# Batch 0 of an RWKV-to-Fourier kernel: fills and table halves on ScalarE, one masked state update per chunk, and a new written-out order

## The chip, the cores and the metric

The kernel runs on one core of a Trainium2 chip. The metric is device time in microseconds of one execution. The engines of the core work side by side, each through its own queue of instructions in order: TensorE (PE in the profile, its weight loads PEld), VectorE (DVE), ScalarE (ACT), GpSimd (POOL) and SyncE (SP), which issues nearly all DMAs.

## The reference

Two layers follow one another. The first is a linear attention with a state that decays channel by channel; the second mixes all tokens and channels of a batch by a two-dimensional Fourier transform (real part), normalises, and applies a two-layer MLP. B, H, S, D = 4, 8, 768, 48.

```
for t in range(S):
    kt, vt, rt, wt = k[:, :, t], v[:, :, t], r[:, :, t], w[:, :, t]
    cur = einsum('bhd,bhe->bhde', u[None] * kt, vt)
    y[:, :, t] = einsum('bhd,bhde->bhe', rt, state + cur)
    state = wt[..., None] * state + einsum('bhd,bhe->bhde', kt, vt)
x = y.transpose(0, 2, 1, 3).reshape(B, S, H * D)        # 4 x 768 x 384
u = x + real(fft(fft(x, axis=1), axis=2))
un = (u - mean(u)) / sqrt(var(u) + 1e-6)                 # over the 384 channels
out = u + maximum(un @ w_ch1, 0) @ w_ch2                 # 384 -> 1536 -> 384
```

## The kernel before, in words

**Tiling.** The tokens of a batch are cut into six chunks of 128, so that there are 24 chunks; chunk c of batch b is called b.c here. A chunk's w, k, r and v come in as four loads of 192 KB each (`in_w`, `in_k`, `in_r`, `in_v`, seven buffers of each), all issued by SP in one row. The attention of a chunk goes: the logarithm of w (`lb`, ACT), cumulative sums of it by matmuls with masks (L567, L571, and per-head totals at L577, PE), exponentials (ACT), r and k times these (`rh`, `kh`, on DVE for batch 0; `kh` on POOL from batch 1 on), transposes (PE) and their eviction (`rtb`, `ktb`, ACT), the 128x128 products (L637, PE), their masking (`ah`, DVE), the new state (L652 and L654, PE; `st`, DVE), the output (L672 and L676, PE), and the diagonal term from r, k, u and v (`rk` twice and `vtd` on POOL, `dc` on DVE; in batch 0 it is added by a float32 matmul at L684). The result goes to `x` (L688 on ACT in batch 0, L690 on DVE later). Two heads share the 128 partitions: the state tile is 128 x 4 x 96, and only the half of each 96 that belongs to the own head may be other than zero.

**Mixing and MLP.** `x` is folded into sums and differences (`xf`), multiplied with cosine and sine tables `cs` and `ss` (L732), evicted to `hcs` (L736), mirrored (`hcr`, POOL), multiplied with the channel tables `dtm` and `dtp` (L749), added to x (L751), normalised (`un`), transposed and evicted (`unt`, L771). Then come the two MLP layers: L790 with its evictions `ht` (L799 on ACT, L795 on DVE), and L809, whose result goes through `osb` (L814, DVE) to the output. L790 needs `w1` and L809 needs `w2`, which POOL loads in two DMAs of 1152 KB.

**Tables.** `cs` and `ss` are made in the kernel: DVE reduces the angles (194 columns for each of three row blocks), ACT takes the sines, and DVE mirrors each quarter with a sign per partition (`sgb`, `sgs`; four tensor_scalar operations in `mirrors`). `tables_end` fills row blocks 3 to 5 from blocks 0 to 2, once copied and once negated (four DVE operations, 576 to 579 columns), and makes `dtm` and `dtp`.

**Order.** Every operation is recorded once with its dependences. `ORDER` is a list of all operation numbers, written out by a planner outside the kernel; each engine executes its own operations in that order, and `BANKS` gives the PSUM bank of each new tile. Waits between engines follow from the dependences. A stalled operation holds all behind it on its engine. Twenty pairs of matmuls without use (L851, "warm") are strewn into PE's row in the first stretch.

Of the kernel before, what the change touches and what calls it, by code (L numbers as in the profile page):

```python
# [75 lines left out]
]  # L76
BANKS = (
    "01023402567432053245243260745603275063543257020560726405702501027615453276601650465325701327363601540235701357"
    "04317420370154237015470231754315236571632451764356437565361014234761032604371461376035427610312521521125761532"
    "65713675431647153265723102752407562716304571641350730473601457632701647546320165460154603546210654106235461676"  # L80
    "0173275410326754104326710543040236745012362"
)
# [203 lines left out]
def bass_rwkv6_finch__then__fnet_fourier_mix_kernel(  # L286
# [119 lines left out]
    def fill(o, val):  # L406
        return lambda e: e.memset(o, val)
# [477 lines left out]
```

## Time and profile before

| | before |
|---|---|
| median of 3 runs | 209.9 us (209.96, 209.9, 208.45) |
| profiled execution, its own time | 208.6 us |
| span of the profile | 206.7 us |
| PE / DVE / ACT / POOL busy | 186.8 / 154.6 / 140.8 / 121.5 us |
| mean granted TensorE clock | 0.989 of full speed |
| loads and stores moved | 26.26 MB |

The span runs from the first to the last instruction; the profiled execution's own time has 1.9 us around it. "Busy" on PE counts the warm matmuls too (L851, 11.1 us in all). In the first quarter of the span PE is not full: in the 40 slices of the page its busy tenths begin 3599957798799999.

### The profile page before, as it was taken

The page shows a single profiled execution, that of the slowest core. Times are in us where ns is not written, and L with a number is a line of the kernel's source. Part 1 is how long each engine was busy: PE and PEld are TensorE (multiplying, and loading weights), DVE is VectorE, ACT ScalarE, POOL GpSimd, SP SyncE. Part 2 cuts the span into 40 slices and gives each one's busy share as a digit, 9 for nine tenths or more (in the row PEclk, how much of TensorE's full clock was granted, in tenths as well). Part 3 has the DMA queues.
Part 4 walks back from the last instruction along what each step waited for, and adds up shares of the span by engine and source line. Part 5 has one row for each costly group of instructions (what it writes and reads, how often), then busy time and mean ns, then how long its engine had stood idle before and what let it go on. Part 6 is the DMA issues. An engine that isn't in the chain of part 4 may idle for free.

```text
span 206.7 us, 4611 instructions
## 1 busy us (share of the span) xinstructions
PE 186.8 (90%) x1760; PEld 116.4 (56%) x1760; DVE 154.6 (75%) x344; ACT 140.8 (68%) x325; POOL 121.5 (59%) x152
## 2 busy tenths in 40 slices
PE   3599957798799999898999999999999999999994
PEld 0255634453466666575666666766566666656652
DVE  7789998387745899999996589999648994823403
ACT  3898843455999997586996695669956613883530
POOL 5777876435479998785999998992011483000000
PEclk9999999799999999999999999999999999999998
DMA  6999999999999999989929910210110101201203
GB/s 119 220 217 205 196 185 166 166 205 203 187 213 217 183 223 203 226 177 233 209 76 186 195 41 3 76 41 0 38 41 0 43 30 50 75 4 38 76 3 114
DMA packets 105273, 26.26 MB, mean 127 GB/s; under 512 B 100257, under 2 KB 104866, under 8 KB 105250
## 3 DMA queue, kind: packets, MB, share of 16 engines
q1 hardware_dynamic: 103298, 23.60, 53.2%
q0 software_dynamic: 1952, 2.36, 7.2%
q8 instruction: 14, 0.23, 0.5%
q14 instruction: 9, 0.07, 0.1%
HBM read 23.59 MB, written 4.72 MB: 137 GB/s over the span
## 4 chain that ended last, share of the span: by engine, by line
PE 41%; DVE 19%; SPq 11%; POOL 10%; ACT 7%; DMA 5%; issue 5%; POOLq 0%; DVEq 0%; ACTq 0%
PE bank L790 14%; PE bank L809 13%; SPq L431 11%; POOL rk L396 5%; DMA in_v<-in_v_dram 5%; DVE ah L642 4%; PE bank L749 3%; DVE xf L396 3%; DVE osb L814 3%; DVE xa L396 2%; DVE st L662 2%; DVE x L690 2%; POOL kh L396 2%; POOL vtd L396 2%; PE bank L637 1%
## 5 line engine op out<-in xcount | busy, mean ns | idle before, releaser
L790 PE MATMUL bank<-unt,w 128*128 128x384 bf16 x288 | 52.9, 326 | 0.6 <-ACT unt L771 0.6
L809 PE MATMUL bank<-w,ht 128*128 128x384 bf16 x288 | 53.1, 326 | 0.0
L799 ACT ACTIVATE ht<-bank 128x384 bf16<-128x384 f32 x80 | 37.0, 497 | 10.2 <-PE bank L790 10.2
L790 PEld LDWEIGHTS bank<-unt,w 128*128 128x128 bf16 x288 | 26.1, 98 | 17.5 <-ACT unt L771 1.0
L809 PEld LDWEIGHTS bank<-w,ht 128*128 128x128 bf16 x288 | 26.8, 98 | 16.1 <-ACT ktb L629 0.2
L642 DVE TENSOR_TENSOR ah<-bank,msk 128x512 bf16<-128x512 f32 x48 | 31.2, 682 | 6.2 <-PE bank L637 6.0
L396 POOL TENSOR_TENSOR vtd<-in_v,dc 128x384 f32<-128x384 f32 x24 | 20.0, 836 | 13.9 <-DVE dc L594 9.0
L396 POOL TENSOR_TENSOR kh<-in_k,e 128x384 bf16<-128x384 f32 x18 | 18.1, 1008 | 15.7 <-ACT e L587 15.7
L396 POOL TENSOR_TENSOR rk<-in_r,in_k 128x384 f32<-128x384 f32 x24 | 24.2, 1008 | 3.5 <-DMA in_r<-in_r_dram 3.2
L396 POOL TENSOR_TENSOR rk<-rk,ub 128x384 f32<-128x384 f32 x24 | 24.2, 1014 | 0.8
L814 DVE SCALAR_TENSOR_TENSOR osb<-bank,rstd,x 128x384 f32<-128x384 f32 x24 | 14.7, 611 | 11.8 <-PE bank L809 11.7
L410 ACT ACTIVATE un<-x,agg 128x384 bf16<-128x384 f32 x24 | 14.5, 617 | 6.9 <-DVE agg L757 6.8
L662 DVE TENSOR_TENSOR st<-bank,e 64x192 bf16<-64x192 f32 x40 | 14.1, 353 | 4.6 <-PE bank L676 2.3
L594 DVE TENSOR_REDUCE dc<-rk 128x8 f32<-128x384 f32 x24 | 13.2, 551 | 5.3 <-POOL rk L396 3.1
L751 DVE TENSOR_TENSOR x<-bank,x 128x384 f32<-128x384 f32 x24 | 12.6, 547 | 5.0 <-PE bank L749 5.0
L629 ACT ACTIVATE ktb<-bank 128x512 bf16<-128x512 bf16 x24 | 14.2, 602 | 2.8 <-PE bank L624 2.7
L627 ACT ACTIVATE rtb<-bank 128x512 bf16<-128x512 bf16 x24 | 14.2, 601 | 2.8 <-PE bank L618 2.4
L602 DVE TENSOR_TENSOR rh<-bank,in_r 128x384 bf16<-128x384 f32 x24 | 13.0, 547 | 3.5 <-ACT bank L573 3.2
L410 ACT ACTIVATE vb<-in_v 128x384 bf16<-128x384 f32 x24 | 12.7, 531 | 2.9 <-DMA in_v<-in_v_dram 2.8
L410 ACT ACTIVATE lb<-in_w 128x384 bf16<-128x384 f32 x24 | 12.6, 528 | 2.6 <-PE bank L567 2.5
L795 DVE TENSOR_SCALAR ht<-bank 128x384 bf16<-128x384 f32 x16 | 8.8, 551 | 7.3 <-PE bank L790 7.1
L587 ACT ACTIVATE e<-bank 128x388 f32<-128x388 f32 (+1 forms) x18 | 9.0, 506 | 7.4 <-PE bank L577 5.9
(116 smaller groups left out, 373.6 us busy)
## 6 DMA issues: line engine op xcount, KB each, us to landing
in_w<-in_w_dram SPq DMA_DIRECT2D x24, 192.0 KB, 3.7
in_k<-in_k_dram SPq DMA_DIRECT2D x24, 192.0 KB, 3.9
in_r<-in_r_dram SPq DMA_DIRECT2D x24, 192.0 KB, 3.8
in_v<-in_v_dram SPq DMA_DIRECT2D x24, 192.0 KB, 3.9
out_dram<-osb SPq DMA_DIRECT2D x24, 192.0 KB, 1.9
w<-in_moe_w_ch_dram POOLq DMA_DIRECT2D x2, 1152.0 KB, 10.6
ht<-in_u_dram SPq DMA_DIRECT2D x1, 1.5 KB
```

The source lines that it names most:

```text
L396: return shared(lambda e: e.tensor_tensor(out=o, in0=a, in1=b, op=f))
L410: return lambda e: e.activation(o, a, f, **kw)
L431: return e.dma_start(INB[n][i][:, :, :], src[n][b, :, c * CH:(c + 1) * CH, :].rearrange("h t d -> t h d"))
L594: op("dve", "dc", lambda e: e.tensor_reduce(out=dc[:, :], in_=rku[:, :, :], axis=mybir.AxisListType.X, op=ALU.add), r=[("RK", i2)], w=[("D ...
L627: op("act", "ev512", lambda e: e.activation(rT[:, :, :].rearrange("p h t -> p (h t)"), psb(trr)[:, 0:512], ACTF.Copy), r=[trr], w=[("RTB", ...
L629: op("act", "ev512", lambda e: e.activation(kT[:, :, :].rearrange("p h t -> p (h t)"), psb(trk)[:, 0:512], ACTF.Copy), r=[trk], w=[("KTB", ...
L642: masked[n] = op("dve", "ah", lambda e, x=x: e.tensor_tensor(out=ah[:, x:H:2, :], in0=ps(ta[x])[:, :].rearrange("p (h t) -> p h t", t=128) ...
L662: op("dve", "st", lambda e, x=x, pr=pr: e.tensor_tensor(out=s_out[pr, :, D * x:D * x + D], in0=ps(tds)[pr, 0:DM].rearrange("p (h d) -> p h ...
L790: ins = e.matmul(ps(t)[:, 0:384], W1[:, m, 128 * j:128 * j + 128], unt[:, m, :], start=(m == 0), stop=(m == NM - 1))
L799: op("act", "ev384", lambda e, j=j, t=t, ht=ht: e.activation(ht[:, j, :], ps(t)[:, 0:384], ACTF.Relu), r=[t], w=[("HT", q % 2, j)])
L809: ins = e.matmul(ps(t)[:, 0:DM], ht[:, j, 128 * x:128 * x + 128], W2[:, j, :], start=(j == 0), stop=(j == NJ - 1))
L814: op("dve", "osb", lambda e, kb=kb, t=t, o=o: e.scalar_tensor_tensor(out=o[:, :], in0=ps(t)[:, 0:DM], scalar=rstd[:, kb:kb + 1], in1=uf[:, ...
```

## The change

1. The zero columns 48 to 63 of every head in `lb`, `rh` and `kh` are filled by ScalarE (a Copy of a broadcast zero, `fill384`) and no longer by GpSimd. The fill of the state tile goes away.
2. In batch 0 the state update becomes one VectorE operation over all 128 partitions and 384 columns (`stm`) in place of two over 64 partitions and 192 columns (`st`). The factor for the half that must be zero is made zero: the totals get a second column per head pair, and a further matmul adds -10000 to the exponent of the entries that don't belong (`totm`, with the new tile `NEGM`).
3. The four mirrors of the tables become tensor_tensor operations, with the sign broadcast as second operand (`mirt`).
4. The four fills of row blocks 3 to 5 go from VectorE to ScalarE (`upa`).
5. `ORDER` and `BANKS` are new throughout.

```diff
     def fills():
-        e = "pool"
         for n, T in (("LB", LBS), ("RH", RHS), ("KH", KHS)):
-            op(e, "fill192", fill(T[:, :, :, D:64].rearrange("p n h d -> p (n h) d"), 0.0), w=[(n, i) for i in range(NB)])
-        op(e, "fill768", fill(STS[:, :, :, :].rearrange("p n h d -> p (n h d)"), 0.0), ...)
+            zero(T[:, :, :, D:64].rearrange("p n h d -> p (n h) d"), NB * H, 64 - D, "fill384", [(n, i) for i in range(NB)], FE[0])
...
+    def zero(o, n, m, kind, w, e="act"):
+        if e == "act":
+            op(e, kind, act(o, ZERO[:, 0:1].unsqueeze(1).to_broadcast([128, n, m]), ACTF.Copy), r=["ZERO"], w=w)
+        else:
+            op(e, kind, fill(o, 0.0), w=w)
...
-            op("dve", "mir", ts(T[:, 0:3, HS:HS - 96:-1], T[:, 0:3, Q:Q + 96], sg[:, :], None, ALU.mult),
+            sgb = sg[:, 0:1].unsqueeze(1).to_broadcast([128, 3, 96])
+            op("dve", "mirt", tt(T[:, 0:3, HS:HS - 96:-1], T[:, 0:3, Q:Q + 96], sgb, ALU.mult),
...
-            op("dve", "up", shared(lambda e, T=T: e.tensor_copy(out=T[:, 3:6, Q:HF], in_=T[:, 0:3, Q:HF])),
-            op("dve", "up", ts(T[:, 3:6, 0:Q], T[:, 0:3, 0:Q], -1.0, None, ALU.mult), r=lo, ...)
+                    op("act", "upa", act(T[:, 3:6, q0:q1], T[:, 0:3, q0:q1], ACTF.Copy, scale=(1.0, -1.0)[x]), r=lo, w=w)
...
+    FE, UPE, MST, HCD = ("act", "pool", "pool", "pool"), ("act", "act"), range(NC), ()
...
                 for h in range(HP):
-                    ins = e.matmul(ps(tci)[:, DM + h:DM + h + 1], L[:, 2 * h:2 * h + 2, :]..., ONE[:, :])
+                    ins = e.matmul(ps(tci)[:, DM + m * h:DM + m * h + m], L[:, 2 * h:2 * h + 2, :]..., ONE[:, 0:m], ...)
+                if mst:
+                    ins = e.matmul(ps(tci)[:, DM:DM + H], IDB[:, :], NEGM[:, :, :].rearrange("p h x -> p (h x)"), start=False, stop=True, ...)
...
+            if mst:
+                op("dve", "stm", lambda e: e.tensor_tensor(
+                    out=s_out[:, :, :].rearrange("p h (x d) -> p h x d", d=D),
+                    in0=ps(tds)[:, 0:DM].rearrange("p (h x d) -> p h x d", d=D, x=2),
+                    in1=we.rearrange("p (h x) -> p h x", x=2).unsqueeze(3).to_broadcast([128, HP, 2, D]), op=ALU.mult),
...
-    66, 7, 0, 3, 1, 6, 8, 38, 67, 2, 36, 68, 5, 9, 39, 69, 70, 10, 22, 102, 16, 37, 103, 17,
...
```

The new order shows at three places. The first is on ScalarE, at the end of batch 0's attention. `vb2<-in_v6` is the bf16 copy of the v of chunk 1.0, the first chunk of the next batch; the rows `x<-` are the outputs of batch 0's chunks, the last of them that of chunk 0.5. Before:

```order
L688 ACTIVATE x<-bank7 128x384
L627 ACTIVATE rtb2<-bank0 128x512
L573 ACTIVATE bank6<-bank6 128x384
L410 ACTIVATE vb2<-in_v6 128x384
L688 ACTIVATE x<-bank2 128x384
L629 ACTIVATE ktb2<-bank5 128x512
L629 ACTIVATE ktb0<-bank0 128x512
L627 ACTIVATE rtb0<-bank7 128x512
L688 ACTIVATE x<-bank0 128x384
```

With the change, from the output of chunk 0.5 on:

```order
L720 ACTIVATE x<-bank3 128x384
L555 ACTIVATE dtp<-bank6,cp 128x384
L594 ACTIVATE bank4<-bank4 128x384
L555 ACTIVATE dtp<-bank3 128x384
L772 ACTIVATE hcs0<-bank5 128x2x193
L553 ACTIVATE dtm<-bank3 128x384
L772 ACTIVATE hcs0<-bank2 128x2x193
L772 ACTIVATE hcs0<-bank1 128x2x193
L553 ACTIVATE dtm<-bank6 128x384
L555 ACTIVATE dtp<-bank6 128x384
L653 ACTIVATE rtb0<-bank2 128x512
L413 ACTIVATE vb2<-in_v6 128x384
```

The copy of v of chunk 1.0 stood ahead of the last two outputs of batch 0; now it stands eleven operations behind the last of them.

The second place is the start of the program, on GpSimd and VectorE. `tc`, `ki`, `ht1` and `tci` are index tables; `tn` and the `ht` rows are the first steps of the angle tables, `sgi` the parity of the partition. GpSimd before, and then with the change:

```order
L413 IOTA ki 128x194
L407 MEMSET kh 128x24x16
L413 IOTA tc 128x6
L407 MEMSET lb 128x24x16
L413 IOTA tci 128x1
L407 MEMSET st 128x768
L407 MEMSET rh 128x24x16
L413 IOTA ht1 128x384
```

```order
L416 IOTA ki 128x194
L416 IOTA tc 128x6
L416 IOTA ht1 128x384
L410 MEMSET xf 128x6x128
L410 MEMSET x 128x18x4
L410 MEMSET xf 128x6x128
L416 IOTA tci 128x1
```

VectorE with the change, at the same place; before, `tn` was followed at once by the five `ht0` rows of the tables:

```order
L403 TENSOR_SCALAR tn<-tc 128x3
L403 TENSOR_SCALAR sgi<-tci 128x1
L403 TENSOR_SCALAR msk<-ht1 128x128
L403 TENSOR_SCALAR idw<-ht1 128x384
L404 TENSOR_SCALAR ht0<-ki,tn 128x194
```

The small table `tci` moved behind three fills on GpSimd, and its reader `sgi`, with two masks behind it, moved ahead of the angle tables on VectorE.

The third place is on GpSimd where the MLP's weights are loaded (the two DMA rows; `vtd3` belongs to chunk 0.3, `rk2` to chunk 0.5, `kh<-in_k6` to chunk 1.0). Before, and then with the change:

```order
L542 DMA w1<-in_moe_w_ch1_dram 128x3x1536
L396 TENSOR_TENSOR xf<-x 128x191
L396 TENSOR_TENSOR vtd3<-in_v3,dc0 128x384
L396 TENSOR_TENSOR rk2<-in_r5,in_k5 128x384
L396 TENSOR_TENSOR rk2<-rk2,ub 128x384
L396 TENSOR_TENSOR kh<-in_k6,e2_0 128x8x48
L396 TENSOR_TENSOR rk0<-in_r6,in_k6 128x384
L544 DMA w2<-in_moe_w_ch2_dram 128x12x384
```

```order
L399 TENSOR_TENSOR rk1<-rk1,ub 128x384
L399 TENSOR_TENSOR xf<-x 128x191
L560 DMA w1<-in_moe_w_ch1_dram 128x3x1536
L399 TENSOR_TENSOR rk2<-in_r5,in_k5 128x384
L562 DMA w2<-in_moe_w_ch2_dram 128x12x384
L399 TENSOR_TENSOR vtd0<-in_v4,dc1 128x384
```

Six GpSimd operations stood between the two weight loads, one of them with a wait for chunk 1.0; now one stands between them. On SyncE, whose row isn't shown, the first two stores of the output move ahead of `in_v` of chunk 2.0; before, they stood behind `in_k` of chunk 2.3 and `in_k` of chunk 2.4.

More of the change, by code (lines that the diff above doesn't have):

```diff
@@ L324, in bass_rwkv6_finch__then__fnet_fourier_mix_kernel @@
     LB, RH, KH = ([T[:, i] for i in range(NB)] for T in (LBS, RHS, KHS))
-    E2 = [sb("e2_%d" % i, [H * D + HP], FP32) for i in range(NB)]
+    E2 = [sb("e2_%d" % i, [H * D + H], FP32) for i in range(NB)]
     VB = [sb("vb%d" % i, [H, D], BF16) for i in range(4)]
@@ L362, in bass_rwkv6_finch__then__fnet_fourier_mix_kernel @@
     NLE = sb("nle", [128], BF16)
-    ONE = sb("one", [1], BF16)
+    ONE = sb("one", [2], BF16)
+    ZERO = sb("zero", [1], FP32)
+    NEGM = sb("negm", [HP, 2], BF16)
+    PM1 = sb("pm1", [2], FP32)
     BEPS = sb("beps", [1], FP32)
@@ L488, in tables @@
         op("act", "table", lambda e: e.preload_act_table_set("natural_log_exp_and_others"), r=[(n, q) for n in ("SSl", "CSl") for q in range(3)], w=["LOGEXP"])
+        for x in range(2):
+            op("dve", "ts1", ts(NEGM[:, :, x], TC[:, 0:1].to_broadcast([128, HP]), 63.5, -1e4, ALU.is_lt if x else ALU.is_gt, ALU.mult),
+               r=["TC"], w=["NEGM%d" % x])
         op("dve", "ts1", ts(SGI[:, :], TCI[:, :], 1, None, ALU.bitwise_and), r=["TCI"], w=["SGI"])
@@ L559, in attention @@
         L = LB[i2]
-        e2, we = E2[i2][:, 0:DM].rearrange("t (h d) -> t h d", d=D), E2[i2][:, DM:DM + HP]
+        mst = n in MST
+        nw = H if mst else HP
+        e2, we = E2[i2][:, 0:DM].rearrange("t (h d) -> t h d", d=D), E2[i2][:, DM:DM + nw]
         rh, kh, vb = RH[i2], KH[i2], VB[n % 4]
@@ L575, in tot @@
             def tot(e):
+                m = 2 if mst else 1
                 for h in range(HP):
-                    ins = e.matmul(ps(tci)[:, DM + h:DM + h + 1],
-                                   L[:, 2 * h:2 * h + 2, :].rearrange("t h d -> t (h d)"), ONE[:, :])
-                return ins
-            op("pe", "tot", tot, r=["ONE", ("LB", i2)], w=[tci])
-        ne = DM if last else DM + HP
+                    ins = e.matmul(ps(tci)[:, DM + m * h:DM + m * h + m],
+                                   L[:, 2 * h:2 * h + 2, :].rearrange("t h d -> t (h d)"), ONE[:, 0:m],
+                                   start=not mst or h == 0, stop=not mst, skip_group_check=True)
+                if mst:
+                    ins = e.matmul(ps(tci)[:, DM:DM + H], IDB[:, :], NEGM[:, :, :].rearrange("p h x -> p (h x)"), start=False, stop=True,
+                                   skip_group_check=True)
+                return ins
+            op("pe", "totm" if mst else "tot", tot, r=["ONE", ("LB", i2)] + (["IDB", "NEGM0", "NEGM1"] if mst else []), w=[tci])
+        ne = DM if last else DM + nw
         if early:
@@ L659, in attention @@
                + ([] if first else [("ST", (c + 1) % 2, 0), ("ST", (c + 1) % 2, 1), "IDB"]), w=[tds])
-            for x in range(2):
+            if mst:
[3 more added lines that the diff above has]
+                    in1=we.rearrange("p (h x) -> p h x", x=2).unsqueeze(3).to_broadcast([128, HP, 2, D]), op=ALU.mult),
+                   r=[tds, ("E2", i2)], w=[("ST", c % 2, 0), ("ST", c % 2, 1)])
+            for x in range(0 if mst else 2):
                 pr = slice(64 * x, 64 * x + 64)
```

36 lines of the change are left out of this document (23 added, 13 removed), and 125 rows, old and new, of the table ORDER.

## The prediction

> **What bounds the kernel now.** I read the busy table first, then the span cut at the first matmul of the MLP (53.9 us) and at the last (203.2), then the waits and the timeline of the stretch before 53.9. Columns of the cut: length, busy us of each engine (instructions), granted clock, DMA share, GB/s.
>
> ```profile
> PE 186.8 (90%) x1760; PEld 116.4 (56%) x1760; DVE 154.6 (75%) x344; ACT 140.8 (68%) x325; POOL 121.5 (59%) x152
> 8.95:43.40 34.45, 28.46 (x306) 16.90 (x305) 27.12 (x62) 21.82 (x52) 23.22 (x29) 0.95 1.08 191
> 53.90:203.20 149.30, 146.59 (x1384) 93.90 (x1385) 109.81 (x236) 106.45 (x247) 87.79 (x102) 1.00 0.46 103
> 53.91 3.10 PE L790 MATMUL bank<-unt,w 128*128 128x384 bf16 x18 [0.60 <-ACT unt L771]
> ```
>
> From the first MLP matmul at 53.91 PE is busy 146.59 of 149.30 us at full clock: that part is PE's own work, and little but less work on PE shortens it. The remaining 3.5 us are the last `osb` and its store. What can move is the start at 53.91. Before it stands batch 0's attention, and there two stalls show:
>
> ```profile
> 26.49 2.40 DVE L400 TENSOR_SCALAR ss<-ss,sgs 128x285 bf16<-128x285 bf16 x2
> 29.03 0.66 PE L732 MATMUL bank<-ss,xf 128*128 128x385 bf16 x3 [2.26 <-DVE ss L400]
> 31.41 0.50 ACT L587 ACTIVATE e<-bank 128x388 f32<-128x388 f32 x1 [3.26 <-PE bank L577]
> 25.47 0.94 POOL L542 DMA_DIRECT2D w<-in_moe_w_ch_dram  x1
> 25.70 10.77 DMA in_v<-in_v_dram
> 36.50 0.52 ACT L410 ACTIVATE vb<-in_v 128x384 bf16<-128x384 f32 x1 [2.76 <-DMA in_v<-in_v_dram]
> 36.92 0.47 ACT L688 ACTIVATE x<-bank 128x384 f32<-128x384 f32 x1
> 39.32 1.29 DVE L642 TENSOR_TENSOR ah<-bank,msk 128x512 bf16<-128x512 f32 x2 [3.27 <-PE bank L637]
> 42.16 0.72 DVE L662 TENSOR_TENSOR st<-bank,e 64x192 bf16<-64x192 f32 x2 [1.03 <-PE bank L676]
> 42.89 0.49 ACT L688 ACTIVATE x<-bank 128x384 f32<-128x384 f32 x1 [4.03 <-PE bank L684]
> ```
>
> First, two mirrors of `ss` hold DVE for 2.40 us, PE waits 2.26 for them and ACT 3.26 behind PE. Second, ACT waits 2.76 us for v of chunk 1.0, a load that took 10.77 us because the first weights were requested at 25.47 beside it; the outputs of chunks 0.4 and 0.5 (36.92 and 42.89) stand behind, and DVE waits 3.27 and 1.03 for what they hold up.
>
> **The change part by part.**
>
> *Start.* The new `sgi` on DVE waits for `tci`, which on POOL now ends behind three fills; the masks, the angle tables, the sines and the first logarithm are queued behind it.
>
> ```profile
> 0.84 0.32 POOL L413 IOTA ki<- 128x194 f32 x1 [0.39 <-POOLq L870]
> 3.06 0.51 POOL L413 IOTA ht<- 128x384 f32 x1
> 8.31 0.75 POOL L407 MEMSET xf<- 128x768 bf16 x1
> 2.04 1.87 DVE L401 TENSOR_SCALAR ht<-ki,tn 128x194 f32<-128x194 f32 x3
> 5.24 0.42 DVE L404 SCALAR_TENSOR_TENSOR ht<-ki,tc,ht 128x194 f32<-128x194 f32 x1
> 5.72 0.59 DVE L400 TENSOR_SCALAR ht<-ht 128x194 int32<-128x194 int32 x3
> 6.05 1.11 POOL L396 TENSOR_TENSOR rk<-in_r,in_k 128x384 f32<-128x384 f32 x1 [2.48 <-DMA in_r<-in_r_dram]
> 8.95 0.94 ACT L410 ACTIVATE lb<-in_w 128x384 bf16<-128x384 f32 x2
> 10.65 0.56 DVE L602 TENSOR_TENSOR rh<-bank,in_r 128x384 bf16<-128x384 f32 x1 [1.51 <-ACT bank L573]
> ```
>
> POOL: 0.84 + 0.3 + 0.1 + 0.51 + 0.75 + 0.15 + 0.75 + 0.1, so `tci` at 3.5. DVE then needs some 0.8 for `sgi` and two masks, and for the tables 9 x 0.22 and 3 x 0.40 at the undisturbed lengths of 5.72 and 5.24 (the three at 2.04 took 0.6 each beside POOL's fills): 7.5, or 8.5 if the `rk` at 6.05 blocks it. Before, the last was done at 6.31. One cosine instead of three then follows on ACT, which takes back 0.7. I take the first logarithm 1.2 us later (bounds 0.3 and 2.0): 10.2 for 8.95, and the first `rh` at 11.9 for 10.65. The three fills on ACT (0.5 each by the 384-column rows of ACT) lie in its idle time before the first sine; POOL's lost fills were no bound.
>
> *DVE's row to the last fold of batch 0.* Before, it is busy 27.84 us in 10.65 to 44.3:
>
> ```profile
> 10.65:44.30 33.65, 27.66 (x309) 16.80 (x306) 27.84 (x63) 20.42 (x49) 22.36 (x28) 0.95 1.08 190
> 25.75 0.82 DVE L506 COPY cs<-cs 128x579 bf16<-128x579 bf16 x1
> 40.52 0.35 DVE L506 COPY ss<-ss 128x579 bf16<-128x579 bf16 x1
> 21.08 0.64 DVE L400 TENSOR_SCALAR cs<-cs,sgb 128x288 bf16<-128x288 bf16 x2
> L662 DVE TENSOR_TENSOR st<-bank,e 64x192 bf16<-64x192 f32 x40 | 14.1, 353 | 4.6 <-PE bank L676 2.3
> L606 DVE TENSOR_TENSOR kh<-bank,in_k 128x384 bf16<-128x384 f32 x6 | 3.2, 547 | 0.3 <-ACT e L585 0.3
> 6.70 0.55 DVE L400 TENSOR_SCALAR idf<-ht 128x128 f32<-128x128 f32 x1
> ```
>
> Out go the four fills of row blocks 3 to 5 (0.82 and three near 0.35: 1.85), the mirrors (0.64 + 2.40 = 3.04), the `rh` and two `st` of chunk 1.0, which now stand behind the fold (0.5 + 0.72), and sign rows of 0.3. A masked update reads as much as a `kh` from PSUM, so 0.55 for 2 x 0.353: 5 x 0.16 = 0.8 less. In come `idf` (0.55) and the two mirrors of `cs`; those of `ss` fall into DVE's idle time before the first `rh`. So 27.84 - 7.2 = 20.6, and with 0.55 and the mirrors 22.6.
>
> The mirrors' price is the open one. A tensor_tensor with all its inputs in SBUF stands in the folds:
>
> ```profile
> L396 DVE TENSOR_TENSOR xf<-xa x9: 350/525/1157, 83.3 to 170.9; 128x193 bf16<-128x193 f32 x9
> ```
>
> (min, median, max in ns.) With 285 columns I bound one mirror at 0.36 and 1.8, the latter the longer `ss` mirror (2.40 less a free 0.6), and take 0.7, near the median. The Trainium skill, page "SBUF — State Buffer", section "Who interferes with whom", says that a DVE instruction with two SBUF inputs contends with a GpSimd instruction that reads SBUF, as the one-input fast modes do, and that the second to come blocks until the first is done. By that rule the rewrite as two-operand operations frees nothing. The fold's 350 to 1157 ns agrees.
>
> *ACT.* Four copies of 576 columns come in, two of them ahead of logarithms:
>
> ```profile
> L629 ACT ACTIVATE ktb<-bank 128x512 bf16<-128x512 bf16 x24 | 14.2, 602 | 2.8 <-PE bank L624 2.7
> L688 ACT ACTIVATE x<-bank 128x384 f32<-128x384 f32 x6 | 2.9, 492 | 5.1 <-PE bank L684 5.0
> ```
>
> From 492 ns for 384 columns and 602 for 512 I get 0.66 each, 2.6 together. The first waits for a mirror on DVE, and behind it `exp` of chunk 0.2 and the logarithm of 0.3 are queued. ACT's busy time of 21.82 (8.95 to 43.4) loses 2.7 for chunk 1.0's operations, which go behind chunk 0.5, and gains 3.2 with one `dtm`: 22.3, from 10.2 on, with 2 us of waits 34.5. So DVE is still the later one, and the copies are hidden.
>
> *Sum to chunk 0.5's output.* DVE: 11.9 + 22.6 = 34.5. Of its 5.8 us of idle time before, 4.3 was the second stall (3.27, and 1.03 behind it), and some 2 stay: 36.5. The in-order rows of two nearly full engines will not mesh perfectly; 0.5 for that. The output of chunk 0.5 starts at **37.0** (bounds 35 and 40.5) for 42.89.
>
> *From there to the first MLP matmul*, 53.91 - 42.89 = 11.0 before.
>
> ```profile
> 50.38 1.15 ACT L410 ACTIVATE un<-x,agg 128x384 bf16<-128x384 f32 x2 [2.07 <-DVE agg L757]
> 46.79 0.36 PE L676 MATMUL bank<-vb,ah 128*128 128x48 bf16 x8
> 52.63 0.33 PE L567 MATMUL bank<-lb,msk 128*128 128x384 bf16 x1
> ```
>
> ACT gets chunk 1.0's five operations into this stretch (2.7) and loses two `dtm`/`dtp` and a logarithm to others (1.9); 2.07 of idle time covers the rest. I take 11.2, so 48.2, that is 5.7 earlier. v of chunk 1.0, due at 36.5 before, is read at about 43, so that the second stall is gone. PE has more left after that point: the output of 1.0 (0.36) and the sums of 1.1 (0.33 and two alike, overlapping), 0.9 in all. So 5.7 - 0.9 = 4.8 us less if PE stays as full: span 206.7 - 4.8 = 201.9, own time 208.6 - 4.8 = 203.8. The three runs lie from 0.15 below to 1.36 above that own time; I add 0.5 and forecast **204.3**.
>
> *Weights and loads.* The first weights wait on POOL behind the fold of chunk 0.1, I estimate until 28 for 25.47; the second follow after one operation, before they came at 33.95:
>
> ```profile
> 33.95 1.07 POOL L544 DMA_DIRECT2D w<-in_moe_w_ch_dram  x1
> 35.92 0.37 SPq L431 DMA_DIRECT2D in_w<-in_w_dram  x1
> 72.28 0.87 SPq L431 DMA_DIRECT2D in_w<-in_w_dram  x1
> 83.46 0.51 ACT L410 ACTIVATE lb<-in_w 128x384 bf16<-128x384 f32 x1
> ```
>
> The loads of 1.1 (35.92) wait for the first weights, so they start 2.5 later, but the DMA engines (share 1.08) only swap the order of the same bytes. Cost nothing, since w of chunk 2.3, issued at 72.28, is read at 83.46. If that cover is gone, see the first rival.
>
> **The rivals.**
>
> 1. *The gain is lost between batch 0's and batch 1's MLP.* PE's 146.59 of 149.30 rests on chunks 1.1 to 2.x being ready. Their loads don't come earlier, and two stores stand ahead of `in_v` of 2.0, waiting for `osb` of batch 0. For it: the DMA share of 1.08 up to 43.4. Against: the cover of 11 us, over twice the gain. If all 4.8 go, own time 208.6, about 208.9 in the runs. Chance 0.19. Half the gain lost (206.5) I count with the forecast.
> 2. *Slower: the port takes more than the stalls gave.* `idf`, both `cs` mirrors and `nidw` stand in DVE's full row where POOL multiplies back to back. If each waits out two of POOL's 1.0 us operations, as the `ss` mirror did (1.8), that is 4 x 1.8 - 2.6 forecast = 4.6 more on DVE, and ACT, whose first copy waits for a mirror, takes its row behind it later by as much again where it is full, some 3 us; 204.3 + 7.6 = 211.9. It decides from 4.8 us on. Against: the median of the folds, 0.53. Chance 0.11.
> 3. *The rows mesh better*, with no idle time beyond the start and no blocked mirror: chunk 0.5's output at 35, own time 201.8, runs near 202. Chance 0.15.
> 4. *The change doesn't do what it says*: the stall on `in_v` of 1.0 stays, since beside both weights it could take twice its 10.77 us, to 47. Then ACT stands still 4 us and more, 208 to 210. Against: v is issued at 25.70, ahead of them. Chance 0.04.
>
> **How the numbers follow.** The forecast has 0.51 (202.7 to 207). A measurement of this kernel tells about 1%, 2.1 us, from no change; so faster means below 207.8: the forecast, the third rival and 0.03 of the first, 0.69. Same: the rest of the first and most of the fourth, 0.19. Slower by over 1%: the second, and a little of the fourth, 0.12. The range takes in the third rival's 202 and the first's 209, and leaves out the second: 201.3 to 209.3.
>
> **What would show it.** Right: the output of chunk 0.5 on ACT near 37 with no wait on `in_v`; the first MLP matmul near 48; PE busy over 97% from there to the end; first logarithm at 10.2; ACT's copies near 0.66. Wrong: `ss` and `cs` mirrors over 1 us on DVE, ACT idle before its first copy, PE idle by several us between 60 and 100 with DVE or a DMA as releaser, or a first logarithm past 11.

## The result, and the profile after

| | before | after |
|---|---|---|
| median, first comparison | 209.93 us (208.45 to 210.88, 4 runs) | 200.94 us (200.73 to 201.28, 4 runs) |
| ratio, with its 95% interval | | 0.9579 (0.9521 to 0.9638) |
| profiled execution, own time / span | 208.6 / 206.7 us | 200.75 / 198.6 us |
| first MLP matmul | 53.91 us | 47.34 us |
| from there to the end of the span | 152.8 us | 151.3 us |

The change gained 9.0 us; the forecast was 5.6 (204.3), and the range began at 201.3. Two later comparisons of the same kernel gave 203.82 (ratio 0.9665, 0.9582 to 0.9749) and 204.87 us (0.9701, 0.9571 to 0.9831); why they differ is part of what follows. The comparisons leave out runs more than 1.5% above a kernel's fastest, which for the kernel before, whose runs spread by 2% and more, is part of its own spread; so the medians below are those of all runs, beside that ratio.

The busy table of the changed kernel:

```profile
PE 185.8 (94%) x1765; PEld 116.3 (59%) x1765; DVE 152.9 (77%) x340; ACT 144.7 (73%) x332; POOL 119.8 (60%) x148
```

Its span cut at the first logarithm, at chunk 0.5's output and at the first and last MLP matmul (columns as in the prediction):

```profile
9.14:37.00 27.86, 24.86 (x276) 15.24 (x277) 26.08 (x52) 21.61 (x52) 20.08 (x23) 1.00 1.07 196
37.00:47.34 10.34, 9.80 (x82) 5.42 (x81) 6.58 (x16) 9.23 (x21) 6.04 (x9) 1.00 1.00 170
47.34:195.10 147.76, 146.31 (x1398) 94.24 (x1399) 112.04 (x244) 107.37 (x249) 88.46 (x104) 1.00 0.52 114
```

PE's timeline at the first MLP matmul:

```profile
47.34 3.57 PE L826 MATMUL bank<-unt,w 128*128 128x384 bf16 x21 [0.51 <-ACT unt L807]
```

PE is now busy 24.86 of 27.86 us in the attention of batch 0 (28.46 of 34.45 before), and from the first MLP matmul on 146.31 of 147.76, so that 1.45 us of idle time are left there for 2.71.

The timeline of the start, of POOL, DVE and ACT:

```profile
5.51 0.74 DVE L407 SCALAR_TENSOR_TENSOR ht<-ki,tc,ht 128x194 f32<-128x194 f32 x2
5.84 1.61 POOL L399 TENSOR_TENSOR rk<-in_r,in_k 128x384 f32<-128x384 f32 x1 [2.61 <-DMA in_r<-in_r_dram]
6.18 0.42 DVE L403 TENSOR_SCALAR ht<-ht 128x194 int32<-128x194 int32 x2
9.09 1.45 DVE L399 TENSOR_TENSOR ss<-ss,sgs 128x288 bf16<-128x288 bf16 x2
9.14 0.94 ACT L413 ACTIVATE lb<-in_w 128x384 bf16<-128x384 f32 x2
10.19 1.20 POOL L399 TENSOR_TENSOR rk<-in_r,in_k 128x384 f32<-128x384 f32 x1
10.46 0.96 DVE L404 TENSOR_SCALAR negm<-tc 128x4 bf16<-128x4 f32 x1
```

The tables on DVE end at 6.6 (6.3 before), and not at 7.5 or 8.5: `rk` came on POOL at 5.84, after DVE's operations at 5.51 had begun, so POOL was held up (1.61 us for about 1.0) and not DVE. At 10.46 it is the other way round: POOL's `rk` was first (10.19), and four columns of `negm` took DVE 0.96 us.

The timeline of POOL, SP and ACT at the weights and at the end of batch 0's attention:

```profile
25.51 0.94 POOL L560 DMA_DIRECT2D w<-in_moe_w_ch_dram  x1
25.93 0.80 SPq L434 DMA_DIRECT2D in_v<-in_v_dram  x1
36.98 0.49 ACT L720 ACTIVATE x<-bank 128x384 f32<-128x384 f32 x1 [0.61 <-PE bank L716]
41.53 0.60 ACT L413 ACTIVATE vb<-in_v 128x384 bf16<-128x384 f32 x1
```

From the view of `in_v`, the time from that request to its landing:

```profile
DMA to landing us min/median/max: 15.1/15.1/15.1
```

The weights are requested at 25.51, not at 28, and v of chunk 1.0 is still 0.42 us behind them. It takes 15.1 us and lands at 41.03; ACT reads it at 41.53. The second stall is gone with 0.5 us to spare.

The last place is the stretch behind the first MLP matmul. Three stretches of the kernel before, the first of them the 15 us from that matmul on:

```profile
53.91:68.91 15.00, 14.99 (x131) 9.47 (x132) 7.86 (x17) 14.16 (x37) 12.66 (x14) 1.00 1.02 202
80.00:90.00 10.00, 9.09 (x121) 6.22 (x120) 9.70 (x18) 6.21 (x13) 7.45 (x9) 1.00 1.04 211
90.00:100.00 10.00, 8.92 (x106) 6.00 (x105) 9.92 (x24) 7.33 (x16) 7.31 (x10) 1.00 0.96 208
```

The same of the changed kernel:

```profile
47.34:62.34 15.00, 14.99 (x133) 9.45 (x134) 9.69 (x23) 14.30 (x37) 11.20 (x12) 1.00 0.99 195
80.00:90.00 10.00, 9.77 (x110) 7.02 (x108) 9.15 (x22) 7.83 (x17) 9.02 (x12) 1.00 0.98 212
90.00:100.00 10.00, 10.00 (x94) 6.41 (x92) 8.93 (x24) 10.00 (x25) 9.62 (x11) 1.00 0.99 213
```

Before, DVE was busy 7.86 us in the 15 us behind the first MLP matmul and full at 80 to 100, where PE lost 0.91 and 1.08 us. After, DVE has 9.69 us in the same 15 us (they lie 6.57 us earlier on the clock), and PE loses 0.23 in the other two.

### The profile page after: what moved, and what is told of

It is laid out like the page before. It is cut to its first block, busy times and chain, and to the rows that moved or that the text cites. A ratio compares the mean times of both kernels' runs of the same rounds, so it can differ in the third digit from the quotient of the medians.

```text
span 198.6 us, 4633 instructions
## 1 busy us (share of the span) xinstructions
PE 185.8 (94%) x1765; PEld 116.3 (59%) x1765; DVE 152.9 (77%) x340; ACT 144.7 (73%) x332; POOL 119.8 (60%) x148
## 4 chain that ended last, share of the span: by engine, by line
PE 54%; DVE 28%; POOL 7%; ACT 5%; DMA 2%; issue 2%; SPq 1%; POOLq 0%; DVEq 0%
PE bank L826 16%; PE bank L845 14%; DVE ah L668 6%; PE bank L785 5%; DVE xf L399 4%; POOL rk L399 4%; PE bank L764 3%; DVE osb L850 3%; PE bank L663 3%; DMA in_r<-in_r_dram 2%; DVE xa L399 2%; PE bank L650 2%; PE bank L644 2%; DVE dc L620 2%; DVE rh L628 2%
## 5 line engine op out<-in xcount | busy, mean ns | idle before, releaser
L826 PE MATMUL bank<-unt,w 128*128 128x384 bf16 x288 | 54.1, 326 | 0.5 <-ACT unt L807 0.5
L845 PE MATMUL bank<-w,ht 128*128 128x384 bf16 x288 | 54.1, 326 | 0.0
L835 ACT ACTIVATE ht<-bank 128x384 bf16<-128x384 f32 x80 | 37.8, 496 | 15.3 <-PE bank L826 15.1
L399 POOL TENSOR_TENSOR rk<-in_r,in_k 128x384 f32<-128x384 f32 x24 | 24.8, 1035 | 6.7 <-DMA in_r<-in_r_dram 6.2
L399 POOL TENSOR_TENSOR vtd<-in_v,dc 128x384 f32<-128x384 f32 x24 | 19.9, 833 | 12.9 <-DVE dc L620 11.9
L399 POOL TENSOR_TENSOR kh<-in_k,e 128x384 bf16<-128x384 f32 x18 | 19.0, 1060 | 2.3 <-ACT e L613 2.3
L399 POOL TENSOR_TENSOR xd<-x 128x385 f32<-128x385 f32 x9 | 9.0, 1004 | 14.6 <-DVE x L722 14.6
L653 ACT ACTIVATE rtb<-bank 128x512 bf16<-128x512 bf16 x24 | 14.7, 611 | 1.4 <-PE bank L644 1.2
L887 PE MATMUL bank<-idw,msk 128*128 128x384 bf16 x40 | 10.9, 380 | 3.9 <-DVE idw L403 3.9
```

The lines of the kernel that those rows point to most:

```text
L399: return shared(lambda e: e.tensor_tensor(out=o, in0=a, in1=b, op=f))
L653: op("act", "ev512", lambda e: e.activation(rT[:, :, :].rearrange("p h t -> p (h t)"), psb(trr)[:, 0:512], ACTF.Copy), r=[trr], w=[("RTB", ...
L826: ins = e.matmul(ps(t)[:, 0:384], W1[:, m, 128 * j:128 * j + 128], unt[:, m, :], start=(m == 0), stop=(m == NM - 1))
L835: op("act", "ev384", lambda e, j=j, t=t, ht=ht: e.activation(ht[:, j, :], ps(t)[:, 0:384], ACTF.Relu), r=[t], w=[("HT", q % 2, j)])
L845: ins = e.matmul(ps(t)[:, 0:DM], ht[:, j, 128 * x:128 * x + 128], W2[:, j, :], start=(j == 0), stop=(j == NJ - 1))
```

## The experiments

### One copy moved back

ScalarE's row of the changed kernel, with `vb` of chunk 1.0 where the kernel before had it, ahead of the output of chunk 0.4:

```diff
 ktb  0.5
+vb   1.0
 x    0.4
 dtm
 x    0.5
 ...
 rtb  1.0
-vb   1.0
```

> The changed kernel with one copy moved back: vb of chunk 1.0 stands ahead of the output of chunk 0.4 in ScalarE's row, as before the change. Theory A (the order of this one copy is most of the gain): in the changed kernel the load of v for chunk 1.0 is issued at 25.93 and takes 15.1 us, so it lands at 41.0; ScalarE would wait there from about 32.6, the output of chunk 0.4 would start at 41.5 for 35.23 and the first MLP matmul some 5 us later, at 52 for 47.34: 205 to 207 us. Theory B (the new operations are the gain, the order little): under 202.5 us.

Measured 209.41 us (207.38 to 212.08, 6 runs) beside 211.69 for before; ratio 0.9879 (0.9711 to 1.0047). Three of the runs lie at 207.4 to 207.7 and three at 211.1 to 212.1; the profile is of one of the latter (211.14). Its timeline on ACT:

```profile
44.76 0.52 ACT L413 ACTIVATE vb<-in_v 128x384 bf16<-128x384 f32 x1 [11.88 <-DMA in_v<-in_v_dram]
```

The stretch of 10 us in which this wait ends:

```profile
40.00:50.00 10.00, 3.89 (x14) 1.98 (x15) 1.71 (x5) 4.60 (x10) 2.28 (x4) 0.50 1.04 188
```

Most of the gain is gone with one copy: the ratio is 0.988 for the 0.958 to 0.970 of the changed kernel's three comparisons. The three faster runs lie just above the 205 to 207 of Theory A. In the profiled one v landed at 44.7 and not at 41; PE stood still, and its granted clock fell to 0.50 in this stretch. Theory B falls as far as it says that the order matters little.

### The two stalls in the kernel before

No operation is changed here, only the rows of POOL and DVE (the weights move by four of POOL's operations; the expectation counts six):

```diff
 POOL:  vtd 0.4              DVE:  dc  0.0
-        w1                  +      sgs, ss mirror, ss mirror
        fold 0.2                    rh  0.1
        vtd 0.3                     rh  0.0
        rk 0.5, rk 0.5              ...
+        w1                  -      sgs, ss mirror, ss mirror
        kh 1.0
```

Both together:

> The kernel before with only its two stalls treated and no operation changed: the two mirrors of ss (and the sign rows they need) stand ahead of the first rh on VectorE, and the first weights' load stands six operations later on GpSimd, about 30 for 25.47 us, so that v of chunk 1.0 travels ahead of it. Theory A (order): the first stall gives up to 2.3 us, the second up to 2.8, together 204.5 to 206.5 for 209.9. Theory B (operations): 208.5 to 211, since nothing is computed in another way.

One each:

> The kernel before with only the first weights' load moved: six operations later in GpSimd's row, about 30 for 25.47 us. If the race of v with the weights is the larger stall (2.8 us in the profile, more in the runs in which PE's granted clock fell): 3.5 to 5 us below before, and its runs no longer spread by 2%. If the mirrors are the larger one: under 2 us below before.

> The kernel before with only the two ss mirrors (and their sign rows) moved ahead of the first rh on VectorE. By the waits 2.3 us less on PE at 29.03, but ScalarE still stands at v of chunk 1.0, which lands no earlier: if that wait only grows by what came earlier, within 1 us of before; if the stalls add up, 2 to 2.5 us below it.

| kernel | median (runs) | before beside it | ratio | first MLP matmul |
|---|---|---|---|---|
| both | 205.45 (204.87 to 206.56, 4) | 211.69 | 0.9786 (0.9686 to 0.9887) | 50.79 |
| weights later | 207.18 (206.36 to 208.5, 10) | 209.85 | 0.9963 (0.992 to 1.0006) | 51.64 |
| mirrors earlier | 210.57 (207.99 to 210.87, 4) | 209.85 | 1.0116 (0.9932 to 1.03) | 54.60 |

The mirrors alone bring nothing that shows. In that kernel's timeline the time reappears in front of v:

```profile
36.57 0.52 ACT L410 ACTIVATE vb<-in_v 128x384 bf16<-128x384 f32 x1 [4.67 <-DMA in_v<-in_v_dram]
```

4.67 us for 2.76: what came earlier only waits longer. With v out of the way the profiled `ss` mirrors count: the first MLP matmul goes from 51.64 to 50.79, and the medians from 207.2 to 205.5 (of two comparisons, so this step is rough). The weights alone took less than the 3.5 expected; their ratio stands for 0.4 per cent and its interval includes no change, the medians stand for 2.7 us, and between these it stays open. Its ten runs stay within about 1%, those of before beside them spread from 206.73 to 212.67, so this race makes at least part of before's spread.

### The race of v with the weights

The changed kernel again, twice, and with both weight loads behind `vtd` of chunk 0.4 in POOL's row, beside it ("late weights" below):

```diff
 POOL:  fold 0.1
-        w1
        rk 0.5
-        w2
        vtd 0.4
+        w1
+        w2
        fold 0.2
```

> The changed kernel unaltered, as the base for the three beside it. In its profile v of chunk 1.0 landed at 41.03 and was read at 41.5, only 0.5 us to spare, while in the graft with the same first stretch it landed at 45.05. Theory E (the landing is decided anew in every run): some runs 2 to 4 us above the others. Theory F (it is settled by the order of issue): all runs 200.7 to 201.4 again.

> The changed kernel with one thing moved: both weight loads stand two or three operations later in GpSimd's row, behind the vtd of chunk 0.4, about 28.3 and 29.3 us, so that v and r of chunk 1.0 (issued by 26.8) are ahead of them. Theory E (the 200.9 of the first comparison and the 203.8 of the second differ by the race of these loads, which a shift of 0.75 us in their issue decides): v lands within 8 us, no wait for it, 200.7 to 201.8 here too. Rival G (the chip of the second comparison moves everything more slowly): 203 and more, as the changed kernel there.

> The changed kernel unaltered, beside the one with late weights. Theory E (two outcomes, by whether r and v of chunk 1.0 land before they are read): each run is either 200.7 to 201.4 with no wait for them, or 202.4 to 204 with waits of 2 to 4 us. Rival G (the chip is slower as a whole): all runs shifted, and the kernel with late weights with them.

> The kernel with late weights once more, beside the changed kernel. Theory E: 200.0 to 200.8 whatever the changed kernel shows on this chip. Rival G: it moves with the changed kernel, at most 0.7 us below it.

| kernel | median (runs) | before beside it | ratio |
|---|---|---|---|
| after, second comparison | 203.82 (202.46 to 203.93, 4) | 211.47 | 0.9665 (0.9582 to 0.9749) |
| late weights | 200.25 (200.1 to 200.66, 4) | 210.54 | 0.9483 (0.9421 to 0.9545) |
| after, third comparison | 204.87 (202.01 to 207.61, 6) | 212.22 | 0.9701 (0.9571 to 0.9831) |
| late weights, beside it | 200.82 (199.86 to 202.47, 6) | 212.22 | 0.9574 (0.9493 to 0.9654) |

The second comparison's timeline: the requests on POOL and SP, the waits on DVE and ACT.

```profile
25.21 0.93 POOL L560 DMA_DIRECT2D w<-in_moe_w_ch_dram  x1
26.68 5.33 SPq L434 DMA_DIRECT2D in_v<-in_v_dram  x1
40.86 0.56 DVE L628 TENSOR_TENSOR rh<-bank,in_r 128x384 bf16<-128x384 f32 x1 [3.69 <-DMA in_r<-in_r_dram]
44.53 0.52 ACT L413 ACTIVATE vb<-in_v 128x384 bf16<-128x384 f32 x1 [1.91 <-DMA in_v<-in_v_dram]
```

The landing of v in it:

```profile
DMA to landing us min/median/max: 17.8/17.8/17.8
```

Up to chunk 0.5's output nothing is later than in the first profile (36.28 for 36.98), but v is requested 0.75 us later, lands 3.4 us later, and r of the same chunk, now requested behind the weights too, is late as well; the first MLP matmul starts at 50.20 for 47.34. With late weights the request of the first weights, on POOL, and the first MLP matmul, on PE, stand in the timeline so:

```profile
29.09 0.94 POOL L560 DMA_DIRECT2D w<-in_moe_w_ch_dram  x1
46.28 3.57 PE L826 MATMUL bank<-unt,w 128*128 128x384 bf16 x21 [0.51 <-ACT unt L807]
```

And the landing of v:

```profile
DMA to landing us min/median/max: 3.7/3.7/3.7
```

3.7 us for 15.1 and 17.8, and 200.3 to 200.8 us in both comparisons, while the changed kernel beside the latter stood at 204.87. Rival G falls: the chip as a whole wasn't slower. Theory E holds in its core, though the runs don't sort into two clean groups. The kernel with late weights beats both kernels: in the comparison that has both it is 4.0 us under the changed one by the medians and 1.3 per cent (2.7 us) by the ratios.

This is not the price of the loads alone, because the move changed a second thing. Two folds of batch 0 on DVE, in the changed kernel's first profile and with late weights:

```profile
28.73 2.06 DVE L399 TENSOR_TENSOR xf<-x 128x193 bf16<-128x193 f32 x2
28.74 0.90 DVE L399 TENSOR_TENSOR xf<-x 128x193 bf16<-128x193 f32 x2
```

In the first POOL works on its own products beside them (`vtd` from 28.51, two folds from 29.31); with late weights it only issues the two weight loads then (29.09 to 31.08). These folds are on the chain that ended last; they are 1.16 us shorter, and the first MLP matmul comes 1.06 us earlier (46.28 for 47.34), though v kept nobody waiting in that first profile. In the seven profiles with late weights this pair took 0.62 to 1.08 us, in the eight others with the changed first stretch 1.36 to 3.33, the longest in the third comparison. No run separates the two effects.

### The operations, one by one

Each part undone in the changed kernel, first as it is:

```diff
 one-operand mirrors (two places alike):
-op("dve", "mirt", tt(T[:, 0:3, HS:HS - 96:-1], T[:, 0:3, Q:Q + 96], sgb, ALU.mult),
+op("dve", "mirt", ts(T[:, 0:3, HS:HS - 96:-1], T[:, 0:3, Q:Q + 96], sg[:, :], None, ALU.mult),
 half tables on VectorE:
-op("act", "upa", act(T[:, 3:6, q0:q1], T[:, 0:3, q0:q1], ACTF.Copy, scale=(1.0, -1.0)[x]), ...)
+op("dve", "up", ... e.tensor_copy(out=T[:, 3:6, Q:HF], in_=T[:, 0:3, Q:HF]) ...)       # x == 0
+op("dve", "up", ts(T[:, 3:6, 0:Q], T[:, 0:3, 0:Q], -1.0, None, ALU.mult), ...)          # x == 1
 two updates per chunk:
-MST = range(NC)
+MST = ()      # and op("pool", "fill768", fill(STS ...)) behind the index tci
```

> The changed kernel with its four mirrors as one-operand scalings (tensor_scalar) again, in the same places. Theory P (the two-operand form is what keeps the mirrors short beside GpSimd): the ss pair takes 2.4 us again for 1.45 and ends at 11.5, the first rh starts 1 us later, the cs mirrors gain nothing: 201.6 to 202.5. Theory N (the form doesn't matter, the place in the idle time did it): 200.6 to 201.4.

> The changed kernel with the four fills of row blocks 3 to 5 back on VectorE in their old form (copies and scalings, 0.35 to 0.82 us each), at the same places in the order. Theory: VectorE's row up to the last fold of batch 0 is the longest, so 1.9 us more on it come out as 1 to 2 us: 202 to 203. Rival: hidden in VectorE's waits in this stretch: 200.6 to 201.4.

> The changed kernel with two half-height state updates per chunk of batch 0 in place of one masked one (and one more fill on GpSimd, in its idle time). Theory: 5 x 0.16 = 0.8 us more on VectorE come out whole, the masking product on PE goes: 201.4 to 202. Rival: hidden: 200.6 to 201.3.

They gave 204.65 (202.86 to 205.76), 202.35 (201.54 to 202.44) and 203.93 us (203.17 to 205.16), 4 runs each, beside 203.82 for the changed kernel and 211.47 for before. They can't be read as prices, because they move the weights and the folds as well. Undoing the half tables looks like a gain, since its slower rows brought the weights behind v, as its timeline shows:

```profile
26.76 0.71 SPq L434 DMA_DIRECT2D in_v<-in_v_dram  x1
27.03 0.93 POOL L564 DMA_DIRECT2D w<-in_moe_w_ch_dram  x1
```

v landed 3.6 us after its request there. With two state updates v came in time too (7.4 us after its request at 26.40), but the pair of folds met POOL's products, and chunk 0.5's output stood at 40.79:

```profile
30.07 3.24 DVE L400 TENSOR_TENSOR xf<-x 128x193 bf16<-128x193 f32 x2
```

So the same edits were made on the kernel with late weights, and a fourth. The order was written for the changed operations, so what these runs give are prices within that order:

```diff
 fills of lb, rh, kh on GpSimd:
-FE = ("act", "pool", "pool", "pool")
+FE = ("pool", "pool", "pool", "pool")
```

> The same with late weights, and the four mirrors as one-operand scalings again. Theory P (the two-operand form is what keeps the mirrors short): 0.8 to 1.2 us above the kernel with late weights alone. Theory N (the form doesn't matter): within 0.4 us of it.

> The same with late weights, and the four fills of row blocks 3 to 5 back on VectorE in their old form. Theory (VectorE's row is the longest up to the last fold of batch 0): 1 to 1.6 us above the kernel with late weights alone; its first MLP matmul stood at 48.47 for 47.34 where v came early. Rival (hidden): within 0.4 us.

> The same with late weights, and two half-height state updates per chunk of batch 0 in place of the masked one. Theory: 0.8 us (5 x 0.16) above the kernel with late weights alone. Second theory (the shifted row meets GpSimd's products: without late weights two folds took 3.24 us together): 2 us and more. Rival (hidden): within 0.4 us.

> The kernel with late weights and the zero fills of lb, rh and kh back on GpSimd, ahead of the index that the masks and tables wait for. Theory (as forecast: VectorE's tables hang on GpSimd's row at the start): about 0.4 us for each of three fills, the first logarithm at 10 for 9.1, the end 0.8 to 1.2 later: 201.1 to 201.5. Rival (slack there): 200.0 to 200.8.

| late weights, and | median (runs) | ratio | above late weights beside it | first logarithm, first MLP matmul |
|---|---|---|---|---|
| nothing else | 200.25 (200.1 to 200.66, 4) | 0.9483 (0.9421 to 0.9545) | | 9.14, 46.28 |
| one-operand mirrors | 200.47 (199.81 to 201.57, 4) | 0.9508 (0.9425 to 0.959) | 0.2 | 9.21, 46.33 |
| half tables on VectorE | 202.31 (201.67 to 203.26, 4) | 0.9581 (0.9513 to 0.9649) | 2.1 | 9.14, 47.87 |
| two state updates | 202.15 (201.7 to 202.54, 4) | 0.9569 (0.9506 to 0.9632) | 1.9 | 10.25, 47.96 |
| fills on GpSimd | 201.65 (201.25 to 202.82, 6) | 0.962 (0.9551 to 0.9688) | 0.8 (of 200.82) | 11.03, 47.38 |

The timeline of the one-operand mirrors:

```profile
9.10 1.17 DVE L403 TENSOR_SCALAR ss<-ss,sgs 128x288 bf16<-128x288 bf16 x2
12.19 0.31 DVE L403 TENSOR_SCALAR cs<-cs,sgb 128x285 bf16<-128x285 bf16 x1
14.34 0.31 DVE L403 TENSOR_SCALAR cs<-cs,sgb 128x288 bf16<-128x288 bf16 x1
```

Theory P falls: in this place the old form is the shorter one (1.17 for 1.45, 0.31 for 0.45), and the end doesn't notice. The two-operand form can wait behind POOL as well. In the second profile of late weights:

```profile
14.54 1.00 POOL L399 TENSOR_TENSOR rk<-rk,ub 128x384 f32<-128x384 f32 x1
14.64 1.22 DVE L399 TENSOR_TENSOR cs<-cs,sgb 128x288 bf16<-128x288 bf16 x1
```

The half tables: two of their four groups on ACT in the changed kernel (last columns: busy us, mean ns, idle before):

```profile
L413 ACT ACTIVATE cs<-cs 128x576 bf16<-128x576 bf16 x1 | 0.8, 762 | 0.0
L413 ACT ACTIVATE cs<-cs 128x579 bf16<-128x579 bf16 x1 | 0.7, 704 | 0.0
```

Two of the four on VectorE, where they were put back:

```profile
L403 DVE TENSOR_SCALAR cs<-cs 128x576 bf16<-128x576 bf16 x1 | 1.1, 1109 | 0.0
L523 DVE COPY ss<-ss 128x579 bf16<-128x579 bf16 x1 | 1.0, 1006 | 0.0
```

With the other two (353 and 345 ns) they hold VectorE 2.8 us there; 1.6 come out at the first MLP matmul and 2.1 at the end, so that row is indeed the long one. Of the 1.9 us for two updates 1.1 arises at the start, not in the updates. The added fill on POOL ran beside DVE's masks, in the timeline of POOL, DVE and ACT:

```profile
3.18 0.73 POOL L411 MEMSET st<- 128x768 bf16 x1
3.34 0.66 DVE L404 TENSOR_SCALAR msk<-ht 128x128 bf16<-128x128 f32 x1
10.25 0.94 ACT L414 ACTIVATE lb<-in_w 128x384 bf16<-128x384 f32 x2
```

(`msk` took 0.22 in the changed kernel.) That leaves 0.8 for the updates, as forecast, if the 1.1 reach the end in full; no run separates the two. With the fills back on GpSimd the index `tci` came at 4.19 for 3.11 and the first logarithm at 11.03, later than the 10 expected; of 1.9 us there only 0.9 to 1.1 were left at the first MLP matmul and 0.8 at the end. So more than 0.8 may belong to the updates.

### The later order

Two grafts of the rows, each tile in its old bank or all banks relabelled alike:

```diff
 h_ab, l_tail:
-ORDER = that of the changed kernel (of late weights)
+ORDER = its first 380 operations, then all others as in the kernel before
 h_ba:
-ORDER = that of the kernel before
+ORDER = its first 395 operations, then all others as in the changed kernel
```

> A graft: the changed kernel up to its first MLP matmul, and from there on every engine's row in the order of the kernel before (same bank for each tile, relabelled). Theory C (the 1.5 us that the stretch behind the first MLP matmul became shorter come from its own new order): 202.2 to 203 us. Theory D (they come from what the first stretch leaves behind, as loads landed and work done ahead): 200.5 to 201.4, as the changed kernel.

> The other graft: the kernel before up to the third block's normalisation just ahead of the first MLP matmul, and from there on the order of the changed kernel. Theory C (the later stretch's own order gives 1.5 us): 208 to 208.9 for 209.9. Theory D (it gives nothing by itself): 209.5 to 210.5. If the whole gain came from the order behind the first MLP matmul, 202 to 204, which neither theory expects.

> The graft again, now on the kernel with late weights: its order up to the first MLP matmul, then that of the kernel before. Theory C (the later order matters): before's rows put the output of chunk 1.0 and the sums of chunk 1.1 ahead of the first MLP matmul, with the waits in them, so it starts 2 to 3 us later than 46.3, and PE's idle time at 80 to 100 us comes back (0.9 and 1.1 of each 10 us): 203 to 205. Theory D (the later order gives nothing by itself): 200 to 201.

The first two gave 209.74 (207.29 to 211.34, 10 runs; 0.9933, 0.987 to 0.9997) and 210.21 us (208.22 to 213.11, 10 runs; 0.9978, 0.9912 to 1.0043) beside 211.69: far from what either theory said of h_ab. v landed at 45.05 there and ACT waited 3.03 us for it, so the race blurred it. For h_ba the medians differ by 1.5 us, as Theory C has it, but the ratio's interval includes no change. Without the race l_tail gave 205.73 us (205.3 to 206.13, 6 runs; ratio 0.9808, 0.9743 to 0.9874) beside 200.82: 4.9 us more, for the later rows alone, and above what Theory C expected. PE's timeline at the start of the MLP:

```profile
47.43 0.37 PE L708 MATMUL bank<-vb,ah 128*128 128x48 bf16 x8 [1.68 <-DVE ah L668]
48.53 0.50 PE L592 MATMUL bank<-lb,nle 128*128 128x384 bf16 x1 [0.72 <-DVE x L722]
49.30 4.34 PE L826 MATMUL bank<-unt,w 128*128 128x384 bf16 x18
```

Two later stretches of l_tail:

```profile
80.00:90.00 10.00, 8.39 (x110) 5.74 (x108) 9.71 (x17) 6.61 (x16) 8.25 (x10) 1.00 0.91 188
90.00:100.00 10.00, 9.62 (x97) 6.29 (x98) 9.94 (x25) 7.98 (x20) 7.54 (x11) 1.00 1.00 212
```

In before's rows the output of chunk 1.0 (its wait for `ah`) and the sums of 1.1 stand ahead of the first MLP matmul, which starts at 49.30 for 46.52. Then 18 matmuls take 4.34 us for 3.10 before, at a granted clock of 0.91 in 50 to 60. And at 80 to 100 PE's idle time is back (1.99 us, for 0.23 and 0.48 in the two profiles of late weights) beside a full DVE. The spans of the profiles say the same of the stretch behind the first MLP matmul, with one exception:

| later rows | span less the start of the first MLP matmul |
|---|---|
| of before, full clock | 152.8 (before), 152.9 (both stalls), 152.9 (weights later) |
| of before, PE idle ahead of it | 154.2 (h_ab), 154.4 (mirrors earlier), 154.5 (l_tail) |
| of the changed kernel | 151.3 (after), 151.6 (second and third comparison), 151.5 and 152.3 (late weights), 151.6 (h_ba) |
| of the changed kernel, one part undone or one copy moved | 151.2 to 152.2 (seven profiles), 153.3 (half tables on VectorE with late weights) |

Theory C holds for the later rows as a whole. What in them does it is open. That DVE is given more work early behind the first MLP matmul isn't enough of a reason: h_ba, with before's first stretch, has PE busy 9.77 us of the 10 that lie 30 to 40 us behind that matmul, although its DVE did less in the first 15 us (6.96 us) than before's (7.86):

```profile
56.38:71.38 15.00, 15.00 (x125) 9.15 (x126) 6.96 (x17) 14.24 (x37) 9.36 (x11) 1.00 0.83 170
86.38:96.38 10.00, 9.77 (x116) 7.18 (x115) 9.14 (x21) 7.72 (x17) 8.76 (x12) 1.00 0.92 196
```

## Why the prediction was right and wrong

- **The bound** was right: PE is full from the first MLP matmul on, and all that the change brought before it (6.57 us) came out.
- **The start** was mis-sized: first logarithm 9.14 for 10.2, first `rh` 11.33 for 11.9. I reckoned with POOL's `rk` blocking the tables (8.5), but DVE was first and POOL was blocked. The 7.5 without it was 0.9 too long as well: `tci` came 0.3 earlier than summed up, and the masks and tables took less. What the start is worth, the fills show: 1.9 us there, 0.8 at the end.
- **DVE's row** came out, by partly opposite errors. The mirrors took 2.7 us in all for 2.8, a masked update 0.54 for 0.55, and chunk 0.5's output stands at 36.98 for 37.0. Yet the row began 0.6 earlier, was busy 23.9 us for 22.6, and kept 1.8 us of idle time for 2.5: misses that cancel, so the hit is partly luck.
- **The rewrite of the mirrors** did nothing: the end moves by 0.2. By the rule in the Trainium skill, page "SBUF — State Buffer", section "Who interferes with whom", a DVE instruction with two SBUF inputs contends with a GpSimd instruction that reads SBUF. By that rule the new form frees nothing, and the `cs` mirror that took 1.22 us beside `rk`, for 0.45, agrees.
- **ACT's copies** are hidden there, as forecast (0.70 to 0.76 for 0.66); back on DVE these fills cost 2.1 us at the end.
- **"Cost nothing" for the weights** was wrong. They were requested at 25.51, not 28, and v stayed behind them. The first comparison missed the stall by 0.5 us, the other two didn't: the fourth rival, given 0.04, came in part. The sum also left out that the place of these loads decides what POOL does beside DVE's folds. In the third comparison the two together were worth 2.7 us by the ratios and 4.0 by the medians.
- **The rest** is the term that took the time out of the range: I carried before's 152.8 over and added 0.9 for PE, 2.4 us more than the 151.3 measured. More of PE's work did move behind the MLP's start (14 more matmuls), but PE was busy no longer there for it (146.31 us for 146.59), and 1.26 us of idle time went. This comes from the new order of the later rows, which l_tail shows by taking it away; which of their places does it stays open. I had read the new order only up to the first MLP matmul. l_tail also gives a loss such as the first rival feared, beside a full DVE and not for want of loads: with the old later order the kernel stands at 205.7.
- **From 11.0 to 11.2** between that output and the MLP: 10.36 measured, 0.84 less.
- **The 0.5 for scatter** was taken from before's runs. Those of the first comparison lie from 200.73 to 201.28; scatter came with the place of the weights, and went with it.

Together: 0.86 us before the first MLP matmul and 2.4 behind it, less 0.25 around the span, make 3.05 on the own time (203.8 for 200.75); 0.3 of the added scatter make up the 3.4 to the median.

## What to carry to other kernels

A load that is read late can still be on the critical path if it is requested a moment behind a large one on another queue; put the large one behind it and compare again, before any part of a change is priced. Stalls in series don't add up: curing the first alone only lengthens the wait at the second. And where the order is new throughout, the stretch that "is full anyway" has to be read as well: here 1.26 of its last 2.71 us of idle time went with the new rows. A move of one load also shifts what its issuing engine does beside the others, so look there too before the gain is put down to the load.

## What the runs showed of the hardware

**Landing by order of request.** v of 192 KB beside weights of 1152 KB took 3.6 us requested 0.27 us ahead of them (7.4 in another profile, 0.55 ahead), 10.8 when 0.23 behind the first (the kernel before), 15.1 at 0.42 and 17.8 at 1.47 behind with the second weights on their way too. The changed kernel's page offers a reason in its count of packets by size:

```profile
DMA packets 105272, 26.26 MB, mean 132 GB/s; under 512 B 100257, under 2 KB 104866, under 8 KB 105250
```

Nearly all packets are under 512 bytes: a load of 192 KB in rows of 48 floats has 1024 pieces of 192 bytes, and 96 such loads make 98304. Between 2 and 8 KB there are 384, as many as `w1` has rows of 3072 bytes (3 x 128). The Trainium skill, page "DMA: Bandwidth & Descriptors", section "Queues, rings and completion order", says that a DMA engine takes turns between queues packet by packet. By that rule, and if the packets counted here are those of the rule, v would get a seventeenth of the bytes beside `w1` and land after it, an estimate from the sizes above. In the changed kernel the first weights landed 12.0 us after their request (at 37.5), v at 41.03 and the second weights 17.8 us after theirs (at 45.2), which agrees. It was argued, not tried.

**Clock and idle PE.** The granted clock was 0.50 in the stretch in which PE was busy 3.89 of 10 us, and 18 MLP matmuls took 4.34 (l_tail), 4.58 (h_ab) and 4.78 us (mirrors earlier) for 3.10 right behind waits of PE, at granted clocks of 0.91, 0.83 and 0.83 at 50 to 60 us: a stall there cost 1.2 to 1.7 us more than its length. Not every stall did: the kernel before has PE busy 8.00 us of the same stretch at 1.00.

**Who comes first on DVE and POOL.** The later one waited: `rk` took 1.61 us behind DVE (about 1.0 alone), `negm` 0.96 (0.16 alone) and `msk` 0.66 (0.22 alone) behind POOL. The last was beside a fill, which reads nothing.
